# The distance table without its weight: each R tile multiplies for itself

## The chip, the cores and the metric

One core of a Trainium2 chip runs the whole program. The metric is the device time of one execution in microseconds (us); a profiled execution also gives the span from the first to the last instruction. TensorE (PE in the rows) does the matrix products and the transposes, VectorE is DVE, ScalarE is ACT, GpSimd is POOL, and SyncE (SP) issues nearly all transfers. PEld is TensorE's load of stationary operands.

## The reference, cut to what matters

Attention with a position bias that a small network computes, then two feed-forward blocks. Only the bias is touched here:

```python
rel = (pos[:, None] - pos[None, :]).astype(np.float32)
psi_rel = np.log1p(np.abs(rel))
psi_i = np.log1p(np.maximum(pos[:, None].astype(np.float32), 1.0))
x = (psi_rel / psi_i)[..., None]
h = np.maximum(x @ w1 + b1, 0.0)          # w1: 1 x 32, hidden units
bias = h @ w2                             # 32 x 8 heads
scores = scores + bias.transpose(2, 0, 1)[None, :, :, :]
```

There are 2 batches, 8 heads, 576 positions and head size 64. After the softmax and the product with v come two blocks on 1152 x 512 rows: 512 to 2048 to 512, and a gated one with 1536.

## The kernel before, in words

The hidden layer depends on the pair of positions only through the distance d, once it is multiplied by psi_i: max(w1·log1p(d) + psi_i·b1, 0). The table `T` (128 partitions x 576) holds log1p(d). Its partitions are 4 rows of positions x 32 hidden units. `w1c` is w1, one value per partition; a transpose on TensorE (`turned`) makes it, and four small products (`norms`) make psi_i·b1 for all 576 rows. `NB1` is minus that and `SC` is that.

The 576 rows are 36 groups of 16. A group n has four R tiles, each 128 x `reach(n)`, from 304 to 576 columns wide: VectorE makes 123 of the 144 tiles as max(T, NB1 column) and ScalarE makes 21 as Relu(T + SC column). GpSimd has a branch for it and gets none. `bias_mm` (B.n in the table of the order, tile `bps`) multiplies the four by w2, `bias_evac` divides by psi_i into `ev`, `bias_store` writes it to the DRAM tables `biasd`, and `bias_load` reads them back, skewed, as the `bias` tile of a unit of attention. The tables are used in the order c = 2, 1, 3, 4, 0, eight groups each (four for c = 4), so nothing of the first softmax starts until groups 16 to 23 are made, stored and loaded.

A unit u of attention is a pair of heads of a tile of 128 positions: scores (S.u, tile `s`), VectorE's sum with the bias and its minimum (line 472, tiles `e` and `m`), ScalarE's exponential (line 483), transposes (T.u, `tps`), copies (`et`) and the product with v (PV.u). A table, ORDER, fixes TensorE's order for all of this by hand, with "W" for matmuls of the identity that keep TensorE at work and have no use else. The order on VectorE, ScalarE and SP is left to a scheduler, whose estimate decides where it puts an instruction. `rawk`, `rawq` and `vs`/`v` are the loads of k, q and v, `kps`/`qps` the transposed k and q in PSUM, `kS` the copy of the former in SBUF.

In `tile_attention_ffn_kernel` the start reads:

```python
            nc.vector.tensor_copy(out=w1c, in_=turned[:, 0, :1])
            nc.vector.tensor_scalar_mul(T, T, w1c)
            nc.vector.tensor_scalar_mul(NB1, norms, -1.0)
            nc.scalar.copy(out=SC, in_=norms)
```

From about 130 us on the feed-forward blocks run; they have no part in the change.

Of the kernel before, what the change touches and what calls it, by code (L numbers as in the profile page):

```python
# [13 lines left out]
ACTF = mybir.ActivationFunctionType  # L14
ALU = mybir.AluOpType
# [53 lines left out]
def kernel(ctx, tc, q, k, v, w1, b1, w2, w_in, w_out, w_gate, w_val, w_out2, rms_g, dtab, ntab, itab, out):  # L69
    nc = tc.nc  # L70
# [21 lines left out]
    w1c = const.tile([128, 1], F32, name="w1c")  # L92
# [11 lines left out]
    def transpose(out, in_):  # L104
        n = in_.shape[0]
        nc.tensor.transpose(out, in_, ident[:n, :n])  # L106
# [143 lines left out]
    if True:  # L250
# [12 lines left out]
        T = smc.tile([128, S], F32, name="T")  # L263
        SC = smc.tile([128, 4 * NG], F32, name="SC")
        INV = smc.tile([128, NG], F32, name="INV")
        NB1 = smc.tile([128, 4 * NG], F32, name="NB1")
# [39 lines left out]
        def load_k(b, p, n):  # L306

            if b == 2:
                a = rawp.tile([128, H, D], F32, tag="rawl", name="rawl", bufs=1)
                for o in range(2):  # L310
                    nc.sync.dma_start(out=a[64 * o:64 * o + 64], in_=rows(k[o, :, 512:576, :]))
            else:
                a = rawp.tile([128, 4, 2, D], F32, tag="rawk", name="rawk", bufs=BUFS["rawk"])
                for h in range(2):
                    gate(a[:1, 0, h, :1], n)
                    nc.sync.dma_start(out=a[:, :, h], in_=k[b, 2 * p + h, :512, :].rearrange("(c s) d -> s c d", c=4))
                a = a.rearrange("p c h d -> p (c h) d")
            raw_t["k", b, p] = a
# [45 lines left out]
        def reach(n):  # L364

            return max(S - 16 * n, 16 * n + 16)

        def bias_R(n, x, engine):
            R = Rp.tile([128, S], F32, tag="R", name="R")
            R_t[n, x] = R  # L370
            R, src, col = R[:, :reach(n)], T[:, :reach(n)], slice(4 * n + x, 4 * n + x + 1)
            if engine == "A":
                nc.scalar.activation(out=R, in_=src, func=ACTF.Relu, scale=1.0, bias=SC[:, col])
            else:
                if engine == "P":
                    nc.gpsimd.tensor_scalar(out=R, in0=src, scalar1=3.4e38, scalar2=NB1[:, col], op0=ALU.min, op1=ALU.max)
                else:
                    nc.vector.tensor_scalar(out=R, in0=src, scalar1=NB1[:, col], scalar2=None, op0=ALU.max)  # L378

        def bias_mm(n):  # L380
            N = reach(n)
# [184 lines left out]
        def warm(n):  # L566

            if not pv_t:
                for z in range(n):
                    nc.tensor.matmul(warm_t[:, z % 4, :], lhsT=ident, rhs=ident, start=True, stop=True)  # L570

        with tc.manual_schedule():
            nc.sync.dma_start(out=T, in_=dtab.to_broadcast([128, S]))
            nc.scalar.dma_start(out=wr, in_=w1.rearrange("o (g k) -> o g k", g=1).to_broadcast([1, 4, 32]))
            nc.sync.dma_start(out=nr, in_=ntab.rearrange("(o g) t -> o g t", o=1))
            nc.scalar.dma_start(out=br, in_=b1.rearrange("(o k) -> o k", o=1))
            nc.sync.dma_start(out=w2s, in_=w2)
            nc.scalar.dma_start(out=INV, in_=itab.rearrange("g (o t) -> g o t", o=1).to_broadcast([16, 8, NG]))
            load_k(0, 0, None)
            load_k(2, 0, None)  # L580

            make_identity(nc, ident)
            nc.gpsimd.memset(W2b, 0.0)
            nc.vector.memset(nb1, 0.0)
            for b in range(B):
                for o in range(2):
                    (nc.gpsimd if b else nc.vector).memset(v4[b][64 * o:64 * o + 64, :, 1 - o, :], 0.0)
            nc.scalar.activation(out=nb1, in_=nb1, func=ACTF.Exp)
            warm(EARLY[0])
            turned = ps_t.tile([128, 4, 128], F32, tag="t", name="turned")  # L590
            transpose(turned[:, 0, :1], wr.rearrange("o g k -> o (g k)"))
            norms = ps_t.tile([128, 4 * NG], F32, tag="t", name="norms", padded_shape=[128, 512])
            for g in range(4):
                nc.tensor.matmul(norms[32 * g:32 * g + 32], lhsT=br, rhs=nr[:, g], start=True, stop=True)
            warm(EARLY[1])
            nc.vector.tensor_copy(out=w1c, in_=turned[:, 0, :1])
            nc.vector.tensor_scalar_mul(T, T, w1c)
            nc.vector.tensor_scalar_mul(NB1, norms, -1.0)
            nc.scalar.copy(out=SC, in_=norms)

# [22 lines left out]
        for i, n in enumerate(n for c in order for n in range(8 * c, min(8 * c + 8, NG))):  # L623
            g = group_key(i)
            z = "z" if i < 8 else ""
            R_eng[n] = "".join(sorted(START[i] if i < 8 else MID[i % len(MID)], key="PDA".index))
            for j, x in enumerate(sorted(range(4), key=lambda x: "PAD".index(R_eng[n][x]))):
                e = R_eng[n][x]
                at(g + (P[z + "rp"] if e == "P" else P[z + "ra"] if e == "A" else P[z + "rd"] * j), ("R", n, x), (), bias_R, n, x, e)
            at(g + P[z + "b"], ("B", n), [("R", n, x) for x in range(4)] + [("cc",)], bias_mm, n)  # L630
            o = 16 * n + 15
            for h, length in enumerate((o, S - o)):
                e = "D" if length <= P[z + "evd"] else "A"
                at(g + P[z + "ev"] + .001 * h, ("EV", n, h), [("B", n)], bias_evac, n, h, e)
            key = g + P[z + "ev"] + .001 + P[z + "st"]
            at(key, ("ST", n), [("EV", n, 0), ("EV", n, 1)], bias_store, n)
            c = n // 8
            stored_key[c] = max(stored_key.get(c, -99), key)
            nth[i] = n, key - 1e-5
# [352 lines left out]
```

## Time and profile before

| what | value |
|---|---|
| time, median of 3 runs | 632.74 us (631.61 to 634.47) |
| the profiled execution | 632.15 us |
| its span | 630.4 us |
| granted TensorE clock, mean | 0.998 |
| busy: PE, PEld | 620.1 us, 526.4 us |
| busy: DVE, ACT, POOL | 442.2 us, 352.3 us, 143.5 us |
| instructions | 11000 |

The span is 1.75 us shorter than the execution's time; what lies around it is the start and the end of the program. TensorE is counted busy nearly throughout, but a matmul that waits inside its pipeline is counted too, so a small wait shows in the starts of its neighbours rather than as idle time.

### The profile page before, as it was taken

To read this page: it belongs to the slowest core of one execution; us is meant where nothing else is said; L and a number is where in the kernel's file an instruction comes from. 1 tells how busy PE (TensorE), PEld (TensorE's weight loads), DVE (VectorE), ACT (ScalarE), POOL (GpSimd) and SP (SyncE) were. 2 spreads that over 40 slices of the span, in tenths; PEclk is the share of its full clock that TensorE was granted. 3 is DMA by queue.
4 is the path that set the end of the run, shared out by engine and by line. 5 is a ranking of instruction groups with operands and counts; after the bars stand their busy time and mean duration, and the time that the engine had idled before them with its cause. 6 is when DMAs were issued, how large, how long until landed. Compare 5 with 4: busy or idle time off the path is not lost.

```text
span 630.4 us, 11000 instructions
## 1 busy us (share of the span) xinstructions
PE 620.1 (98%) x4185; PEld 526.4 (84%) x4185; DVE 442.2 (70%) x820; ACT 352.3 (56%) x733; POOL 143.5 (23%) x114
## 2 busy tenths in 40 slices
PE   8999999999999999999999999999999999999996
PEld 4456766767779999999999898999999999999996
DVE  5967686547656998988826799878777652497712
ACT  6778877879775655555425555654444431254411
POOL 1000001101210433333300133423323330032500
PEclk9999999999999999999999999999999999999999
DMA  8999565378101433443300223534343430164201
GB/s 193 265 243 285 171 185 157 106 202 281 39 2 36 149 124 128 133 132 115 122 34 0 76 101 127 166 96 122 117 134 100 151 117 0 35 210 130 96 0 51
DMA packets 73569, 77.73 MB, mean 123 GB/s; under 512 B 31659, under 2 KB 58283, under 8 KB 73516
## 3 DMA queue, kind: packets, MB, share of 16 engines
q1 hardware_dynamic: 73362, 77.00, 40.8%
q8 instruction: 33, 0.54, 0.3%
q14 instruction: 20, 0.16, 0.1%
q10 hardware_dynamic: 154, 0.02, 0.0%
HBM read 63.76 MB, written 13.25 MB: 122 GB/s over the span
## 4 chain that ended last, share of the span: by engine, by line
PE 92%; DVE 3%; DMA 2%; ACT 1%; issue 1%; SPq 1%; DVEq 0%; ACTq 0%
PE h L777 40%; PE ya L822 18%; PE yb L822 9%; PE s L459 6%; PE pv L522 6%; PE tps L106 6%; PE bps L389 4%; DVE R L378 1%; DMA bias<-biasd 1%; PE rps L106 1%; PE qps L106 1%; PE xnT L106 1%; DMA T<-in_dtab_dram 1%; DMA rawq<-in_q_dram 1%; DVE wm L164 0%
## 5 line engine op out<-in xcount | busy, mean ns | idle before, releaser
L176 POOL TENSOR_TENSOR wl<-wm,wh 128x512 fp32r<-128x512 f32 x85 | 125.7, 1479 | 301.7 <-ACT wh L143 200.8
L168 DVE SCALAR_TENSOR_TENSOR wm<-raw,wm 128x512 int32<-128x512 int32 x85 | 121.5, 1430 | 0.9
L786 ACT CAST gh<-r 128x384 fp32r<-128x384 f32 x84 | 43.2, 514 | 112.4 <-DVE r L809 68.5
L777 PE MATMUL h<-nh,wh 128*128 128x384 f32 x288 | 97.3, 338 | 0.0
L777 PE MATMUL h<-nh,wl 128*128 128x384 f32 x288 | 96.7, 336 | 0.0
L777 PE MATMUL h<-nl,wh 128*128 128x384 f32 x288 | 96.4, 335 | 0.0
L472 DVE CUSTOM_DVE_ANT_0 e<-s,bias 128x576 f32<-128x576 f32 x72 | 51.9, 754 | 28.4 <-PE s L459 17.9
L483 ACT ACTIVATE e<-e,m 128x576 f32<-128x576 f32 x72 | 55.6, 775 | 17.9 <-DVE m L472 17.7
L777 PE MATMUL h<-xh,wh 128*128 128x384 f32 x192 | 65.4, 341 | 0.0
L777 PE MATMUL h<-xh,wl 128*128 128x384 f32 x192 | 64.7, 337 | 0.0
L777 PE MATMUL h<-xl,wh 128*128 128x384 f32 x192 | 64.4, 336 | 0.0
L809 DVE TENSOR_TENSOR r<-r,h 128x384 f32<-128x384 f32 x36 | 19.9, 553 | 63.3 <-PE h L777 63.3
L164 DVE SCALAR_TENSOR_TENSOR wm<-raw,wm 128x512 int32<-128x512 int32 x85 | 59.7, 704 | 2.8
L789 DVE TENSOR_TENSOR gl<-r,gh 128x384 fp32r<-128x384 f32 x84 | 46.6, 554 | 16.2 <-ACT gh L786 16.2
L154 ACT ACTIVATE wm<-raw 128x512 f32<-128x512 f32 x84 | 56.4, 673 | 0.8 <-DMA raw<-in_moe_w_val_dram 0.8
L777 PEld LDWEIGHTS h<-nh,wh 128*128 128x128 f32 x288 | 54.1, 188 | 2.3 <-DVE nl L886 0.9
L797 ACT ACTIVATE r<-h,half_c 128x384 f32<-128x384 f32 x48 | 27.8, 579 | 49.7 <-PE h L777 49.7
L777 PEld LDWEIGHTS h<-nl,wh 128*128 128x128 f32 x288 | 54.1, 188 | 1.4
L777 PEld LDWEIGHTS h<-nh,wl 128*128 128x128 f32 x288 | 54.0, 188 | 0.0
L805 ACT ACTIVATE r<-h 128x384 f32<-128x384 f32 x36 | 17.7, 493 | 64.9 <-PE h L777 64.9
L143 ACT CAST wh<-wm 128x512 fp32r<-128x512 f32 x85 | 52.3, 617 | 0.9 <-DVE wm L168 0.8
L378 DVE TENSOR_SCALAR R<-T,NB 128x336 f32<-128x336 f32 (+17 forms) x123 | 47.4, 448 | 4.6 <-PE bps L389 4.4
(109 smaller groups left out, 1103.5 us busy)
## 6 DMA issues: line engine op xcount, KB each, us to landing
raw<-in_moe_w_out_dram SPq DMA_DIRECT2D x33, 512.0 KB, 3.5
biasd<-ev SPq DMA_DIRECT2D x36, 295.5 KB, 3.8
raw<-in_moe_w_in_dram SPq DMA_DIRECT2D x18, 512.0 KB, 3.6
raw<-in_moe_w_gate_dram SPq DMA_DIRECT2D x18, 512.0 KB, 3.4
bias<-biasd SPq DMA_DIRECT2D x15, 576.0 KB, 4.7
raw<-in_moe_w_val_dram SPq DMA_DIRECT2D x16, 512.0 KB, 3.4
bias<-biasd SPq DMA_DIRECT2D x10, 288.0 KB, 4.1
rawk<-in_k_dram SPq DMA_DIRECT2D x16, 128.0 KB, 3.2
```

The lines of the kernel that those rows point to most:

```text
L106: nc.tensor.transpose(out, in_, ident[:n, :n])
L143: nc.scalar.copy(out=hi, in_=m)
L154: nc.scalar.activation(out=m, in_=raw[:, :, 1].bitcast(F32), func=ACTF.Abs, scale=held[0] if held else 2.0 ** -112)
L164: nc.vector.scalar_tensor_tensor(out=m, in0=raw[:, :, 0], scalar=29, in1=m, op0=ALU.logical_shift_right, op1=ALU.bitwise_or,)
L168: nc.vector.scalar_tensor_tensor(out=m, in0=raw[:, :, 1], scalar=-0x80000000, in1=m, op0=ALU.bitwise_and, op1=ALU.bitwise_or,)
L176: nc.gpsimd.tensor_tensor(out=lo, in0=m, in1=hi, op=ALU.subtract)
L378: nc.vector.tensor_scalar(out=R, in0=src, scalar1=NB1[:, col], scalar2=None, op0=ALU.max)
L472: nc.vector.tensor_tensor_reduce(out=e_t[u][:, a, :].rearrange("p (z j) -> p z j", z=2), in0=s[:, :, :SH], in1=bt[u][:, a, :].rearrange("p ...
L483: nc.scalar.activation(out=e_t[u][:, a, :], in_=e_t[u][:, a, :], func=ACTF.Exp, scale=-1.0, bias=m_t[t][:, h:h + 1], accum_out=sum_t[t][:, ...
L777: nc.tensor.matmul(ps, lhsT=w[wz][:, c * 128:(c + 1) * 128], rhs=x[xz][:, c, :], start=(i == 0), stop=(i == 11),)
L789: nc.vector.tensor_tensor(out=gl, in0=g, in1=gh, op=ALU.subtract)
L822: nc.tensor.matmul(y_t[ph, n, t], lhsT=g[gz][:, t * 128:(t + 1) * 128], rhs=w[wz], start=(f == 0 and i == 0), stop=(f == F - 1 and i == 2),)
```

## The change

The multiplication of the whole table by `w1c` at the start goes. Each R tile takes the product into its own instruction: on VectorE multiply by `w1c` and then the maximum with the NB1 column, both operands one value per partition; on ScalarE the scale of the activation is `w1c` instead of the constant 1. GpSimd's branch is written likewise, and is not used. Everything else is the same in the source.

```diff
             if engine == "A":
-                nc.scalar.activation(out=R, in_=src, func=ACTF.Relu, scale=1.0, bias=SC[:, col])
+                nc.scalar.activation(out=R, in_=src, func=ACTF.Relu, scale=w1c, bias=SC[:, col])
             else:
                 if engine == "P":
-                    nc.gpsimd.tensor_scalar(out=R, in0=src, scalar1=3.4e38, scalar2=NB1[:, col], op0=ALU.min, op1=ALU.max)
+                    nc.gpsimd.tensor_scalar(out=R, in0=src, scalar1=w1c, scalar2=NB1[:, col], op0=ALU.mult, op1=ALU.max)
                 else:
-                    nc.vector.tensor_scalar(out=R, in0=src, scalar1=NB1[:, col], scalar2=None, op0=ALU.max)
+                    nc.vector.tensor_scalar(out=R, in0=src, scalar1=w1c, scalar2=NB1[:, col], op0=ALU.mult, op1=ALU.max)
...
             nc.vector.tensor_copy(out=w1c, in_=turned[:, 0, :1])
-            nc.vector.tensor_scalar_mul(T, T, w1c)
             nc.vector.tensor_scalar_mul(NB1, norms, -1.0)
```

TensorE's order is the same to the row. VectorE, ScalarE and SP get another order in places. On VectorE, where the first softmax begins (line 472 is the sum with the bias, the row after it its minimum; NB_116 is `NB1`; kS_138 and kS_139 are batch 0 and 1), the program before has:

```order
22 L378 TENSOR_SCALAR R<-T,NB_116 128x352 x4
23 L378 TENSOR_SCALAR R<-T,NB_116 128x336 x3
24 L350 COPY kS_138<-kps 128x512
25 L378 TENSOR_SCALAR R<-T,NB_116 128x400 x2
26 L472 ISA e,m<-s,bias 128x576
27 L472 ISA m 128x1
28 L378 TENSOR_SCALAR R<-T,NB_116 128x400
29 L472 ISA e,m<-s,bias 128x576
```

and the changed program has, at the same place:

```order
21 L378 TENSOR_SCALAR R<-T,w1c,NB_116 128x352 x4
22 L378 TENSOR_SCALAR R<-T,w1c,NB_116 128x336 x3
23 L350 COPY kS_138<-kps 128x512
24 L472 ISA e,m<-s,bias 128x576
25 L472 ISA m 128x1
26 L378 TENSOR_SCALAR R<-T,w1c,NB_116 128x400
27 L472 ISA e,m<-s,bias 128x576
28 L472 ISA m 128x1
```

Two R tiles that stood ahead of the first sum with the bias now stand behind it.

On SP, around the last stores of the first bias table and its first loads (biasd_74 is the table c = 2, biasd_73 is c = 1; vs_140 and vs_141 are v of batch 0 and 1), the program before has:

```order
9 L330 DMA v_142<-in_v_dram 64x4x64
10 L316 DMA rawk<-in_k_dram 128x4x64 x2
11 L418 DMA biasd_74<-ev 16x8x591 x4
12 L316 DMA rawk<-in_k_dram 128x4x64 x2
13 L418 DMA biasd_74<-ev 16x8x591 x4
14 L330 DMA v_142<-in_v_dram 64x4x64
15 L316 DMA rawk<-in_k_dram 128x4x64 x4
16 L444 DMA bias<-biasd_74 128x576 x2
17 L444 DMA bias<-biasd_74 128x2x576 x2
```

and the changed program:

```order
9 L330 DMA v_142<-in_v_dram 64x4x64 x2
10 L316 DMA rawk<-in_k_dram 128x4x64 x2
11 L418 DMA biasd_74<-ev 16x8x591 x4
12 L316 DMA rawk<-in_k_dram 128x4x64 x2
13 L418 DMA biasd_74<-ev 16x8x591 x3
14 L330 DMA vs_141<-in_v_dram 128x4x64
15 L418 DMA biasd_74<-ev 16x8x591
16 L418 DMA biasd_73<-ev 16x8x591
17 L330 DMA vs_140<-in_v_dram 128x4x64
18 L316 DMA rawk<-in_k_dram 128x4x64 x4
19 L444 DMA bias<-biasd_74 128x576 x2
20 L444 DMA bias<-biasd_74 128x2x576 x2
```

One load of v moved far ahead, and two loads of v and the first store of the table c = 1 moved ahead of the k loads and of the first bias loads.

## Rows read from the trace of the kernel before

**Rows 1.** The page, busy time of each engine, share of the span, instructions.

```profile
PE 620.1 (98%) x4185; PEld 526.4 (84%) x4185; DVE 442.2 (70%) x820; ACT 352.3 (56%) x733; POOL 143.5 (23%) x114
```

**Rows 2.** The chain that ended last, 0 to 60 us: start, duration, what.

```profile
16.47 2.72 DVE R L378 x8
...
25.96 6.85 DMA bias<-biasd
...
32.94 0.76 DVE e L472
...
33.76 1.91 PE s L459 x8
```

**Rows 3.** Timeline of VectorE, 4 to 24 us: start, duration, instruction, idle before.

```profile
4.71 0.52 DVE L597 TENSOR_SCALAR T<-T,w1c 128x576 f32<-128x576 f32 x1 [0.45 <-DMA T<-in_dtab_dram]
5.15 0.30 DVE L598 TENSOR_SCALAR NB<-norms 128x144 f32<-128x144 f32 x1
...
7.68 1.94 DVE L378 TENSOR_SCALAR R<-T,NB 128x304 f32<-128x304 f32 x6 [0.66 <-PE bps L389]
11.40 0.69 DVE L350 COPY kS<-kps 128x512 f32<-128x512 f32 x1 [1.79 <-PE kps L106]
12.01 11.80 DVE L378 TENSOR_SCALAR R<-T,NB 128x336 f32<-128x336 f32 x35
```

**Rows 4.** Timeline of TensorE, 19 to 23 us.

```profile
19.32 1.45 PE L389 MATMUL bps<-R,W2b 128*32 128x400 f32 x8 [0.54 <-DVE R L378]
...
21.35 0.91 PE L389 MATMUL bps<-R,W2b 128*32 128x416 f32 x8
22.18 1.09 PE L106 MATMUL kps<-ident,rawk 128*128 128x128 f32 x8
```

**Rows 5.** VectorE by shape: count, busy, mean ns, idle before.

```profile
L378 DVE TENSOR_SCALAR R<-T,NB 128x576 f32<-128x576 f32 x7 | 3.3, 514 | 0.1
...
L378 DVE TENSOR_SCALAR R<-T,NB 128x304 f32<-128x304 f32 x6 | 1.9, 374 | 0.7 <-PE bps L389 0.7
```

**Rows 6.** VectorE line 163, a shift by an immediate: ns min/median/max.

```profile
L163 DVE TENSOR_SCALAR wm<-wm x85: 409/420/1105, 150.8 to 594.0; 128x512 int32<-128x512 int32 x85
```

**Rows 7.** ScalarE out of PSUM: scale by an immediate, by a column.

```profile
L359 ACT ACTIVATE q<-qps 128x512 f32<-128x512 f32 x7 | 4.2, 595 | 0.5 <-PE qps L106 0.5
...
L412 ACT ACTIVATE ev<-bps,INV 128x512 f32<-128x512 f32 x1 | 0.7, 665 | 0.0
```

**Rows 8.** Timeline of ScalarE, 5 to 12 us.

```profile
5.79 3.26 ACT L373 ACTIVATE R<-T,SC 128x320 f32<-128x320 f32 x7
...
10.97 0.60 ACT L359 ACTIVATE q<-qps 128x512 f32<-128x512 f32 x1 [0.17 <-PE qps L106]
```

**Rows 9.** Timeline of SP's queue, 20 to 25 us.

```profile
20.23 0.69 SPq L330 DMA_DIRECT2D v<-in_v_dram  x1
22.87 2.02 SPq L316 DMA_DIRECT2D rawk<-in_k_dram  x4
```

**Rows 10.** Windows before and after the end of the stores, us, busy of each engine, clock, DMA share, GB/s.

```profile
20.00:23.00 3.00, 3.00 (x26) 1.55 (x24) 3.00 (x9) 2.00 (x6) 0.00 (x0) 1.00 0.96 302
23.00:24.00 1.00, 0.92 (x11) 0.19 (x9) 1.00 (x4) 0.94 (x4) 0.00 (x0) 1.00 0.21 55
```

**Rows 11.** R tiles on VectorE by window: us, busy (count), clock, DMA share, GB/s.

```profile
60.00:70.00 10.00, 6.24 (x14) 1.00 1.02 321
...
80.00:90.00 10.00, 8.07 (x18) 1.00 0.66 190
```

**Rows 12.** Timelines behind these bursts: VectorE's sums, TensorE's next scores.

```profile
68.01 0.75 DVE L472 CUSTOM_DVE_ANT_0 e<-s,bias 128x576 f32<-128x576 f32 x1
...
69.68 1.24 PE L459 MATMUL s<-kS,q 64*128 64x288 f32 x8
...
90.13 0.75 DVE L472 CUSTOM_DVE_ANT_0 e<-s,bias 128x576 f32<-128x576 f32 x1
...
90.76 1.41 PE L459 MATMUL s<-kS,q 64*128 64x288 f32 x8
```

## The prediction

> **What bounds the kernel now.** I read the page first: TensorE is counted busy for 620.1 of 630.4 us [rows 1], so a change pays or costs only where it moves the instructions that TensorE waits for. The chain that ended last says where that is early on: up to 19 us it runs through R tiles on VectorE, then through TensorE and a load of the bias of 6.85 us, then VectorE's sum at 32.94, which lets TensorE's next scores start at 33.76 [rows 2]. The timeline of VectorE shows why. It waits 1.79 us for a transposed k, copies it at 11.40, and then makes 35 R tiles in 11.80 us without a gap [rows 3]. TensorE follows close behind: its products with 400 columns at 19.32 waited 0.54 us for an R tile, and those with 416 columns start at 21.35 [rows 4]. Those are tiles 22 to 24 and 25 to 28 of the 35 (before them stand 2 of 336 columns, 4 each of 352, 368 and 384, 3 of 368 and 4 of 384). From 33.76 on TensorE has nearly no idle time, and the R tiles left are made beside it.
>
> **The change part by part.** The first term is the multiplication that goes: one instruction of 0.52 us at 4.71. NB1 was made behind it from 5.15, so the R tiles can start at most 0.52 us earlier. This gives nothing. What it shortens ends in the idle 1.79 us ahead of the copy at 11.40 [rows 3], and that copy waits for k and not for the table. If that cover were gone, the gain would be at most these 0.52 us.
>
> The second term is the longer R tile on VectorE, 123 of them. No row has two column operands in one instruction, so I bound it. From 304 columns (374 ns) to 576 columns (514 ns) a tile grows by 140 ns over 272 columns, 0.515 ns per column [rows 5]. At 512 columns that line gives 481 ns with one column operand. Line 163, of the same 512 columns in SBUF, with an immediate instead, has a median of 420 ns [rows 6]. So a column operand costs about 61 ns. The lower bound for a second one is nothing, if both are fetched together; the upper one is 61 ns, plus half of the rate if the second operation halves it (the third rival). I take 60 ns: the nearest row prices an operand by itself, and nothing in the trace shows two fetched for the price of one. VectorE overlaps neighbours by the same 0.08 us whatever they are (the copy at 11.40 lasts 0.69 and the next tile starts 0.61 after it [rows 3]), so the 60 ns go into the distance from tile to tile in full.
>
> Where that lies: the six tiles from 7.68 take 0.36 us more, inside the 1.79 us of idle time. The copy at 11.40 stays where it is. Then tile 28 of the run that starts at 12.01 ends 28 x 0.060 = 1.7 us later, and with it the products with 416 columns [rows 3, 4]. What is late next: the transposes of k at 22.18 come behind them in TensorE's order, the four k loads at 22.87 wait for those to free their buffers, and the bias loads stand behind these on SP's queue [rows 4, 9]. So the load of 25.96, the sum of 32.94 and the scores of 33.76 [rows 2] all move by 1.7 us. Nothing absorbs it on the way, since this run of tiles is on the chain.
>
> The third term is later bursts, where TensorE has little idle time to give. Between 60 and 70 us there are 14 R tiles, 0.84 us more [rows 11]; the second sum behind them ends at 68.76 and TensorE's next scores start at 69.68 [rows 12], so 0.92 us of room covers that, barely. Between 80 and 90 us there are 18, 1.08 us more; the second sum behind them ends at 90.88, inside the group of scores that began at 90.76 and needs its buffer [rows 11, 12]. There is no room, so up to 1.1 us could come through. Other tiles and two waits of VectorE on TensorE stand in that burst, so I take 0.8, between 0 and 1.3 with the few tiles around 105 us.
>
> The fourth is ScalarE's 21 tiles. There a column operand for the scale shows as 665 against 595 ns, 70 ns [rows 7]. Seven of the tiles start at 5.79, so what follows comes 0.5 us later at most; ScalarE waits 0.17 us ahead of the copy of q at 10.97 [rows 8], and the rest delays only work that stands ahead of VectorE's later run. The other 14 are spread over 100 us. I take nothing, and 0.5 as the upper end.
>
> The fifth is the order. On SP, two loads of v (128 x 256 x 4 bytes, 0.13 MB each) and one store of bias (16 x 8 x 591 x 4 bytes, 0.30 MB) now stand ahead of the k loads and so of the first bias loads, 0.56 MB in all. SP sits idle from 20.92 to 22.87 [rows 9], which covers their issue. The transfers themselves find the engines at 0.21 in the microsecond after 23 us, and at 302 GB/s before it [rows 10]: 0.79 x 302 GB/s takes 0.24 MB, and the other 0.32 MB take 1.1 us. With the k loads 1.7 us later by the second term that is covered. If the second term is nothing, it is not. On VectorE two R tiles stand behind the first sum now instead of ahead of it. That sum waits for the bias load, so this at most hides their own time. I take nothing for both. No wait is new: `w1c` is written before NB1 is, and every R tile waited for NB1 already.
>
> The sum against the profiled execution's own time, 632.15: 632.15 - 0 + 1.7 + 0.8 + 0 + 0 = 634.65, say 634.7 us. That execution lies 0.6 us under the median of the runs shown, 632.74; I leave the forecast at 634.7, 0.3% over the median.
>
> **The rivals.** First, the second operand is free on VectorE. For it: two operands of one instruction may be fetched side by side, and the trace says nothing against it. Then only the fifth term is left, 0 to 1.1 us, and the time is 632.2 to 633.3, the same as before.
>
> Second, the late tiles cost more than I count. In the bursts of rows 11 VectorE's sums, ScalarE's exponentials and TensorE's scores wait for each other in a ring, and a delay in it can come back once per unit instead of once per burst. If both bursts pass on their 0.84 and 1.08 us and the ring doubles what comes through, that is 3.8 us beside the 1.7, near 637.5. Against it speaks the room of 0.92 us at 68.76 [rows 12].
>
> Third, the tile with two operations falls to half its rate. This ends on the other side, slower than a measurement's noise. By the row of 0.515 ns per column it would add as much again: with 378 columns in the mean of the first 28 tiles, 0.195 us each on top of 0.060, so 7.1 us at 33.76 instead of 1.7, and in the bursts 14 x 0.33 - 0.92 = 3.7 and 18 x 0.35 = 6.3 us. That is 639 with nothing of the bursts and 649 with all; about 644. It decides from 0.05 us per tile on top of the operand, since 28 of those make 1.4 us more at the first softmax and 634.7 passes 635.9. The rows have only one operation at this rate, so they can't exclude it.
>
> [...] No run here shows a wide tile with two operations.
>
> Fourth, faster by more than the noise. The sum ahead of two R tiles and the earlier store of the table c = 1 would have to clear more than 3.2 of the 10.3 us in which TensorE is idle in the whole span [rows 1]. The order on TensorE is fixed and the bias load is behind the k loads in both programs, so I see no place for it.
>
> **How the numbers follow.** The forecast 0.55, the free operand 0.24, the later waits 0.11, the halved rate 0.07, faster 0.03. A measurement here can tell about 0.5%, 3.2 us, from no change: 629.6 to 635.9. The range starts at 631.7, under the free operand by half a microsecond for the spread of the runs, and ends at 638.5, which takes in the upper ends of the third and fourth terms (634.7 + 0.5 + 0.5) and the second rival. It leaves out the halved rate, the faster case and the edges of the others, about 2 in 10. Of the forecast a fifth lies over 635.9 (0.11), with most of the second rival (0.09) and all of the third (0.07): slower 0.27. Faster 0.03, the same 0.70.
>
> **What would show it.** R tiles on VectorE of 434 ns at 304 columns and 574 ns at 576 columns, with the same slope, and the run behind the copy at 11.40 growing from 11.80 to about 13.9 us, show the second term. The products with 416 columns should start near 23.0, the k loads near 24.5, the bias load land near 34.5, and the scores of 33.76 come near 35.4. Behind that, the distance from these scores to the first matmul of the feed-forward block should grow by less than 1.3 us. Tiles as long as before show the first rival; then the load of the bias tells whether the moved transfers cost anything. A steeper slope than 0.515 ns per column shows the third. The prediction is wrong if TensorE's waits grow at a place that holds no R tile, for then it is the order on SP or ScalarE that decides and not the tile.

## The result, and the profile after

The changed kernel takes 636.8 us in the median of four runs (636.26 to 637.55), against 632.62 us for the kernel before beside it: a ratio of 1.0067, with a 95% interval of 1.0047 to 1.0087. It is 4.2 us slower. The profiled execution took 636.82 us with a span of 635.0 us, 4.6 us more than the span of before.

The page, busy time of each engine:

```profile
PE 619.8 (98%) x4185; PEld 526.6 (83%) x4185; DVE 449.3 (71%) x819; ACT 353.8 (56%) x733; POOL 143.3 (23%) x114
```

TensorE is as busy as before [rows 1], so all of the loss is new idle time on it. VectorE works 7.1 us more. By shape (count, busy us, mean ns, idle before):

```profile
L378 DVE TENSOR_SCALAR R<-T,w1c,NB 128x576 f32<-128x576 f32 x7 | 3.9, 608 | 0.0
...
L378 DVE TENSOR_SCALAR R<-T,w1c,NB 128x304 f32<-128x304 f32 x6 | 2.3, 434 | 0.6 <-PE bps L389 0.6
```

A tile of 304 columns takes 434 instead of 374 ns [rows 5]. The mean of the seven of 576 columns is raised by one long tile; those of 560 columns, with a mean of 565 ns (506 before), are 59 ns longer. Over all widths the means differ by 57 to 62 ns at 14 of 18; the other four, between 52 and 94, hold single long tiles. The slope over the columns is unchanged (0.512 ns per column from 304 to 560 columns, 0.516 before), so this is a price per instruction. Timeline of VectorE (start, duration, what, idle before):

```profile
4.80 0.31 DVE L597 TENSOR_SCALAR NB<-norms 128x144 f32<-128x144 f32 x1 [0.55 <-PE norms L594]
...
11.74 0.69 DVE L350 COPY kS<-kps 128x512 f32<-128x512 f32 x1 [1.97 <-PE kps L106]
12.35 13.85 DVE L378 TENSOR_SCALAR R<-T,w1c,NB 128x336 f32<-128x336 f32 x35
...
65.67 3.58 DVE L378 TENSOR_SCALAR R<-T,w1c,NB 128x512 f32<-128x512 f32 x7
69.17 0.30 DVE L410 TENSOR_SCALAR ev<-bps,INV 128x95 f32<-128x95 f32 x1
```

The 35 tiles take 13.85 instead of 11.80 us [rows 3], 59 ns more each. The wait ahead of the copy is still there, longer by 0.18 us. Timeline of TensorE:

```profile
23.14 1.07 PE L389 MATMUL bps<-R,W2b 128*32 128x416 f32 x8
24.14 1.09 PE L106 MATMUL kps<-ident,rawk 128*128 128x128 f32 x8
...
30.21 0.63 PE L106 MATMUL kps<-ident,rawk 128*128 128x128 f32 x4 [0.59 <-DMA rawk<-in_k_dram]
...
32.73 0.75 PE L459 MATMUL s<-kS,q 64*128 64x288 f32 x2 [0.56 <-DVE m L472]
33.80 1.23 PE L459 MATMUL s<-kS,q 64*128 64x288 f32 x6 [0.33 <-DVE m L472]
...
36.16 1.77 PE L459 MATMUL s<-kS,q 64*128 64x288 f32 x8
...
69.62 0.63 PE L106 MATMUL rps<-ident,rb 128*128 128x128 f32 x4 [0.49 <-DVE ev L410]
...
72.55 0.66 PE L106 MATMUL tps<-ident,e 128*128 128x128 f32 x4 [0.36 <-ACT et L504]
...
89.91 1.18 PE L389 MATMUL bps<-R,W2b 128*32 128x288 f32 x16 [0.68 <-DVE ev L410]
...
112.24 1.15 PE L389 MATMUL bps<-R,W2b 128*32 128x280 f32 x16 [0.94 <-ACT ev L412]
```

The products with 416 columns start 1.8 us later than in [rows 4], and the scores of 33.76 [rows 2] are now those of 36.16, 2.4 us later. Behind them the slip grows at four waits of TensorE: at 69.62, 89.91 and 112.24 for an evacuation `ev` of the bias products, and at 72.55 for ScalarE's copy `et`. The three of `ev` in the trace of before:

```profile
66.74 0.63 PE L106 MATMUL rps<-ident,rb 128*128 128x128 f32 x4
...
85.80 1.18 PE L389 MATMUL bps<-R,W2b 128*32 128x288 f32 x16
...
107.57 3.73 PE L389 MATMUL bps<-R,W2b 128*32 128x280 f32 x48 [0.44 <-ACT ev L412]
```

So the slip grows from 2.4 us to 2.9 at the first, about 3.4 behind the wait for `et` (the scores of 69.68 [rows 12] come at 73.13), 4.1 and 4.7 us, and stays there. SyncE's queue before, the same queue after, VectorE's first sum with the bias before, and pieces of the chain that ended last after:

```profile
25.00 2.03 SPq L444 DMA_DIRECT2D bias<-biasd  x4
```

```profile
23.63 0.37 SPq L330 DMA_DIRECT2D vs<-in_v_dram  x1
24.83 2.89 SPq L316 DMA_DIRECT2D rawk<-in_k_dram  x4
27.81 1.99 SPq L444 DMA_DIRECT2D bias<-biasd  x4
```

```profile
28.48 0.75 DVE L472 CUSTOM_DVE_ANT_0 e<-s,bias 128x576 f32<-128x576 f32 x1
```

```profile
27.81 4.07 DMA bias<-biasd
31.91 0.76 DVE e L472
```

The k loads are issued 2.0 us later than in [rows 9], and the four bias loads behind them 2.8 us later. The chain runs through a bias load as before, but not through the same one of the four. In [rows 2] it is the third, issued at 25.96, for which VectorE's third sum waits until 32.94. Here it is the first, issued at 27.81: the first sum, which ran at 28.48 before, waits for it until 31.91. TensorE's scores at 32.73 and 33.80 wait for the minima `m` of the first two sums, and those of 36.16 follow without another wait. TensorE's transposes of k wait for their load too, until 30.21, but the scores behind them then wait 0.56 us more for `m`.

About 0.3 us of these differences need not be an effect of the change. TensorE's transposes of q wait for a load, and start at 10.30 in the profiled execution of before, at 10.64 in this one, and between 10.46 and 10.95 in every experiment, with the old tiles and order too.

### The profile page after: what moved, and what is told of

It reads as the page before. It is cut to its first block, busy times and chain, and to the rows that moved or that the text cites. A ratio compares the mean times of both kernels' runs of the same rounds, so it can differ in the third digit from the quotient of the medians.

```text
span 635.0 us, 11006 instructions
## 1 busy us (share of the span) xinstructions
PE 619.8 (98%) x4185; PEld 526.6 (83%) x4185; DVE 449.3 (71%) x819; ACT 353.8 (56%) x733; POOL 143.3 (23%) x114
## 4 chain that ended last, share of the span: by engine, by line
PE 90%; DVE 3%; ACT 3%; DMA 2%; issue 1%; SPq 1%; DVEq 0%; ACTq 0%
PE h L776 40%; PE ya L821 18%; PE yb L821 9%; PE s L459 6%; PE pv L522 6%; PE tps L106 5%; PE bps L389 3%; ACT ev L412 1%; ACT e L483 1%; DVE e L472 1%; PE qps L106 1%; DMA rawq<-in_q_dram 1%; DMA bias<-biasd 1%; PE xnT L106 1%; PE rps L106 1%
## 5 line engine op out<-in xcount | busy, mean ns | idle before, releaser
L472 DVE CUSTOM_DVE_ANT_0 e<-s,bias 128x576 f32<-128x576 f32 x72 | 51.9, 754 | 26.6 <-PE s L459 17.5
L378 DVE TENSOR_SCALAR R<-T,w1c,NB 128x336 f32<-128x336 f32 (+17 forms) x123 | 55.1, 512 | 3.7 <-PE bps L389 3.6
```

What stands on the lines that cost most here:

```text
L378: nc.vector.tensor_scalar(out=R, in0=src, scalar1=w1c, scalar2=NB1[:, col], op0=ALU.mult, op1=ALU.max)
L472: nc.vector.tensor_tensor_reduce(out=e_t[u][:, a, :].rearrange("p (z j) -> p z j", z=2), in0=s[:, :, :SH], in1=bt[u][:, a, :].rearrange("p ...
```

## The experiments

Four theories. **Operand:** the second column operand costs 60 ns on each of VectorE's tiles, and that is the loss. **Operation:** the second operation costs it. **Order:** the rows that the scheduler moved cost it. **ScalarE:** its scale column costs it. All kernels were timed in five rounds. Differences are given by the ratio to the kernel before, times 632.6 us. This ratio is not the quotient of the two medians and can differ from it by some 0.1%.

To part price from order, I wrote the steps of the attention stage into a table in the order in which the engines ran them (a gated load and `x_ri` are cut into their single instructions). With the table of one kernel and the tile code of the other, every engine runs the rows of one in the order of the other.

```diff
-        with tc.manual_schedule(engines={mybir.EngineType.PE}):
-            emit(P["man"], 100)
+        with tc.manual_schedule():
+            for z in STEPS:
...
+                fn(*args)
+                done.add(name)
```

**The control**, the old tiles in the old order. 

> The kernel before, with the steps of its attention stage written out in the order in which its engines ran them, so that no scheduler chooses: every engine has the same rows as before. A control for the next two. Both theories: the time of the kernel before, 632.6 us, within 0.3%. If it is further off, writing the order out costs something of its own (extra waits), and the next two are read against this kernel alone.

Measured: 632.61 us, ratio 1.0000 (0.9984 to 1.0015). Writing the order out costs nothing that shows.

**The new tiles in the old order.**

```diff
-                nc.scalar.activation(out=R, in_=src, func=ACTF.Relu, scale=1.0, bias=SC[:, col])
+                nc.scalar.activation(out=R, in_=src, func=ACTF.Relu, scale=w1c, bias=SC[:, col])
...
-                    nc.vector.tensor_scalar(out=R, in0=src, scalar1=NB1[:, col], scalar2=None, op0=ALU.max)
+                    nc.vector.tensor_scalar(out=R, in0=src, scalar1=w1c, scalar2=NB1[:, col], op0=ALU.mult, op1=ALU.max)
...
-            nc.vector.tensor_scalar_mul(T, T, w1c)
```

> The changed kernel's instructions (distance table not multiplied, each R tile with the weight's column), in the kernel before's order on VectorE, ScalarE, SyncE and TensorE. Theory, that the second column operand's 60 ns on each VectorE tile is the whole loss: 636 to 637.5 us, all of the +4.2. Rival, that the scheduler's new order (bias loads later on SyncE, two ScalarE copies behind the exponentials) makes the later half: 634.5 to 635.2, only the +2.4 of the first 34 us.

Measured: 636.01 us, ratio 1.0057 (1.0040 to 1.0073), 3.6 us (2.5 to 4.6). The tiles alone make nearly the whole loss. TensorE's timeline at the scores of 33.76 and the products of 107.57:

```profile
36.33 1.24 PE L467 MATMUL s<-kS,q 64*128 64x288 f32 x8
...
111.80 3.73 PE L397 MATMUL bps<-R,W2b 128*32 128x280 f32 x48 [0.63 <-ACT ev L420]
```

**The old tiles in the new order**: the control with the other table. 

> The other way round: the kernel before's instructions (table multiplied once, one column operand) in the changed kernel's order. Theory (the operand is the loss): 632.2 to 633.4 us, no difference from before. Rival (the order makes the later half): 634.5 to 635.5. If order and operand each cost only together, both of these kernels come out near 633 and neither theory holds.

Measured: 636.28 us, ratio 1.0057 (1.0039 to 1.0076), 3.6 us (2.5 to 4.8). So the order alone makes nearly the whole loss as well, though part of it goes with TensorE's clock: in four of its six executions the mean granted clock is 0.993 to 0.996, and they took 636.05 to 638.26 us; the two at 1.00 took 634.75 and 635.31. My theory and its rival both missed this: each was to get its part, and each gets nearly all of it. SyncE's queue and TensorE's timeline in this kernel:

```profile
23.50 0.93 SPq L322 DMA_DIRECT2D rawk<-in_k_dram  x2
24.52 0.53 SPq L426 DMA_DIRECT2D biasd<-ev  x1
25.14 0.54 SPq L338 DMA_DIRECT2D vs<-in_v_dram  x1
25.78 1.47 SPq L322 DMA_DIRECT2D rawk<-in_k_dram  x2
```

```profile
30.94 0.63 PE L106 MATMUL kps<-ident,rawk 128*128 128x128 f32 x4 [2.53 <-DMA rawk<-in_k_dram]
...
35.99 1.51 PE L467 MATMUL s<-kS,q 64*128 64x288 f32 x8
```

No tile is longer here, and still the transposes of k wait 2.53 us for a load, because the last k load is issued at 26.6 instead of 24.4 us; the bias loads stand behind it in the queue. The scores of 33.76 come at 35.99.

**Two operations with one column operand**, in the old order.

```diff
-                    nc.vector.tensor_scalar(out=R, in0=src, scalar1=NB1[:, col], scalar2=None, op0=ALU.max)
+                    nc.vector.tensor_scalar(out=R, in0=src, scalar1=1.0, scalar2=NB1[:, col], op0=ALU.mult, op1=ALU.max)
```

> The kernel before with each VectorE R tile as two operations, a product with the constant 1.0 and then the maximum with the column; the table is still multiplied once. One column operand as before, same order on every engine. Theory (the column operand costs 60 ns, the operation nothing): 632.3 to 633.0 us, and tiles of 374 ns at 304 columns. Rival, that the second operation is what costs 60 ns: 636 to 637 us, and tiles of 434 ns.

Measured: 632.55 us, ratio 1.0000 (0.9986 to 1.0015). By shape:

```profile
L378 DVE TENSOR_SCALAR R<-T,NB 128x576 f32<-128x576 f32 x7 | 3.3, 513 | 0.1
...
L378 DVE TENSOR_SCALAR R<-T,NB 128x304 f32<-128x304 f32 x6 | 1.9, 372 | 0.8 <-PE bps L389 0.8
...
L373 ACT ACTIVATE R<-T,SC 128x512 f32<-128x512 f32 x1 | 0.7, 718 | 0.0
```

513 and 372 ns are the old times [rows 5]. The second operation adds nothing to them, so the 57 to 62 ns come with the column operand. The slope is the old one too: 0.518 ns per column with two operations, 0.515 with one [rows 5].

Where do operand and order cost? The next four cut both at the scores of 33.76.

**The operand on VectorE's first 55 tiles alone, and on its last 68 alone** (U is the scaled table, T the unscaled one; for the second, `> 55`).

```diff
-            nc.vector.tensor_scalar_mul(T, T, w1c)
+            nc.vector.tensor_scalar_mul(U, T, w1c)
...
+                    if len(vec) <= 55:
+                        nc.vector.tensor_scalar(out=R, in0=raw, scalar1=w1c, scalar2=NB1[:, col], op0=ALU.mult, op1=ALU.max)
+                    else:
+                        nc.vector.tensor_scalar(out=R, in0=src, scalar1=NB1[:, col], scalar2=None, op0=ALU.max)
```

> The old order on every engine; the first 55 R tiles of VectorE (those made before its first sum) take the unscaled table and the weight's column, the other 68 and ScalarE's 21 the scaled table as before. Theory, that the operand's loss has two places, about 2.2 us up to the scores of 33.76 and about 1.9 us in the bursts behind 60 us: 634.5 to 635.3 us, scores of 33.76 2 us later and no further slip behind. Rival, that the later slip only follows from the early one: 636 us, as with all tiles.

> The same with the other 68 VectorE tiles instead (those made after the first sum). Theory of two places: 634.0 to 634.8 us, scores of 33.76 unmoved, the products of 66.74, 85.80 and 107.57 later by 0.6 to 1.9 us. Rival (the later slip only follows from the early one): 632.3 to 633 us. My forecast's third term would say 633.3.

Measured, the first 55: 634.20 us against 632.83, ratio 1.0010 (0.9997 to 1.0023), 0.6 us (-0.2 to 1.5). TensorE's timeline:

```profile
23.16 1.07 PE L403 MATMUL bps<-R,W2b 128*32 128x416 f32 x8
...
36.08 1.91 PE L473 MATMUL s<-kS,q 64*128 64x288 f32 x8 [1.02 <-DVE m L486]
```

In the profiled execution the scores come 2.3 us later, up to 0.4 of it by the load of q, and nothing is added behind them. The chain that ended last runs as in [rows 2], with the same bias load issued 2.0 us later:

```profile
27.95 7.18 DMA bias<-biasd
35.26 0.76 DVE e L486
```

By the ratio the early part is smaller than that, and not safely told from nothing. The granted clock accounts for much of this. Of the 35 executions of before timed beside this kernel, 23 have a mean granted clock of 0.998 or more and took 631.49 to 633.30 us; the other 12 took 633.45 to 635.44. Of this kernel's 12 only one is below 0.998, and the other eleven took 633.15 to 635.16. Among those at 0.998 or more, the medians differ by 1.7 us.

Measured, the last 68: 634.72 us, ratio 1.0026 (1.0011 to 1.0041), 1.6 us (0.7 to 2.6); 2.0 us among the executions at 0.998 or more. VectorE's and TensorE's timelines:

```profile
62.75 4.03 DVE L390 TENSOR_SCALAR R<-T,w1c,NB 128x512 f32<-128x512 f32 x8
66.70 0.30 DVE L424 TENSOR_SCALAR ev<-bps,INV 128x95 f32<-128x95 f32 x1
```

```profile
67.15 0.63 PE L106 MATMUL rps<-ident,rb 128*128 128x128 f32 x4 [0.62 <-DVE ev L424]
...
86.58 1.18 PE L403 MATMUL bps<-R,W2b 128*32 128x288 f32 x16 [0.29 <-DVE ev L424]
...
109.06 3.73 PE L403 MATMUL bps<-R,W2b 128*32 128x280 f32 x48 [0.63 <-ACT ev L426]
```

Here the scores of 33.76 stand at 33.38, 0.4 us early. Then `rps` starts 0.4 us late, the products of 85.80 come 0.8 and those of 107.57 come 1.5 us late: 0.8 + 0.4 + 0.7, 1.9 us in all. The later slip needs no early one. The rival, that the late slip follows from the early one, falls.

**The new order up to the scores of 33.76 alone, and behind them alone** (old tiles; the table is put together from the two). 

> The kernel before's instructions; the changed kernel's order up to the scores of 33.76, the old one behind: only SyncE's queue and the tiny copies that gate two loads differ (two loads of v stand ahead of two k loads and two bias stores). Theory, that these loads delay the k loads behind them: 634.5 to 635.2 us, k loads landing 2 to 3 us later. Rival, that SyncE's order costs nothing, and the loss is ScalarE's and VectorE's order later: 632.3 to 633 us.

> The kernel before's instructions; the old order up to the scores of 33.76, the changed kernel's behind. Theory (SyncE's order early 2.2 us, the rest 1 us): 633.2 to 634.0 us. Rival (the loss is ScalarE's and VectorE's order behind 34 us): 635 to 636.3 us.

Measured, up to 34 us: 634.91 us, ratio 1.0022 (1.0008 to 1.0037), 1.4 us (0.5 to 2.3). Only SyncE's queue and two gating copies differ there, so the moved transfers do cost: 1.3 us between the five executions at 0.998 or more and those of before. In the other seven the clock is lower (0.993 to 0.997). Measured, from 34 us on: 634.38 us, ratio 1.0020 (1.0007 to 1.0033), 1.3 us (0.4 to 2.1). ScalarE's and TensorE's timelines in the second kernel:

```profile
70.42 0.24 ACT L512 COPY et<-tps 128x128 f32<-128x128 f32 x1
70.56 0.58 ACT L555 COPY rt<-rps 128x512 f32<-128x512 f32 x1
71.04 1.07 ACT L512 COPY et<-tps 128x512 f32<-128x512 f32 x2
```

```profile
70.71 0.66 PE L106 MATMUL tps<-ident,e 128*128 128x128 f32 x4 [0.19 <-ACT et L512]
...
87.78 1.18 PE L397 MATMUL bps<-R,W2b 128*32 128x288 f32 x16 [0.38 <-DVE ev L418]
```

ScalarE's copy `rt` now stands behind two exponentials and a copy `et`, and TensorE's transposes wait for `et`. The products of 85.80 wait for VectorE's `ev`, the place at which they also wait for the longer tiles.

By their ratios the halves add up to 2.2 us for the tiles and 2.7 for the order, where the whole is 3.6 each time. By the executions at 0.998 or more it is 1.7 and 2.0, 3.7 us, for the tiles, where the whole is 3.5 (five executions), and 1.3 and 1.9, 3.2 us, for the order, where the whole is 2.5 (two executions). So nothing shows that the halves feed each other.

**ScalarE's 21 tiles alone** (edit as above, on ScalarE's line). 

> The old order; only ScalarE's 21 R tiles take the unscaled table with the weight's column as their scale, VectorE's 123 the scaled table. Forecast's fourth term: nothing, at most 0.5 us, so 632.3 to 633.3 us; the tiles longer by 70 to 100 ns. Rival, that ScalarE's tiles are part of the loss: 634 us or more.

Measured: 632.46 us against 632.26, ratio 0.9997 (0.9986 to 1.0009). By shape:

```profile
L382 ACT ACTIVATE R<-T,SC,w1c 128x512 f32<-128x512 f32 x1 | 0.8, 807 | 0.0
```

807 against 718 ns in the kernel with two operations; 89 to 98 ns over the shapes, 92 in the mean, and no time lost.

**The multiplication taken out alone.**

```diff
-            nc.vector.tensor_scalar_mul(T, T, w1c)
```

> The old order and the old tiles without the multiplication of the table, so that the output leaves out the weight. Forecast's first term: it ends in idle time, 632.3 to 633.0 us, and VectorE's wait ahead of its copy at 11.40 longer by what was saved. Rival, that the 0.5 us come through: 632.0 us or less in the median, which five rounds may just tell.

Measured: 632.89 us, ratio 1.0005 (0.9992 to 1.0018). VectorE's timeline:

```profile
12.35 0.69 DVE L358 COPY kS<-kps 128x512 f32<-128x512 f32 x1 [2.97 <-PE kps L106]
```

VectorE is through with the tiles ahead of this copy at 9.38 instead of 9.61, and what is saved ends in the wait for k. (Most of the wait's 1.2 us over [rows 3] is not that: 0.5 come from the load of q and some from TensorE's transposes at half speed, which the last section shows.)

**Four buffers for k**, with the old tiles and with the new ones, both in the old order but for two k loads that stand one bias store earlier on SyncE.

```diff
-BUFS = dict(rawk=3, rawq=2,
+BUFS = dict(rawk=4, rawq=2,
```

> The kernel before with four buffers instead of three for the loads of k (the steps in the old order; on SyncE two k loads then stand one bias store earlier). Theory, that the loads at 22.87 wait for transposes that wait for VectorE's tiles, and that the scores of 33.76 hang on that: 631 to 632 us. Rival, that the bias loads behind them need the last bias store at 24.5 anyway and the queues are full there: 632.3 to 633 us, or slower where the earlier k loads delay the bias stores.

> The changed kernel's instructions in the old order with four k buffers, so that the four k loads no longer wait for transposes behind VectorE's R tiles. If the early loss goes through those k loads, as my second term had it, it shrinks: 634.2 to 635.2 us, the later 1.9 us being what stays. If it goes through the products and the bias stores alone: 635.6 to 636.5 us, as with three buffers.

Measured: 632.59 us with the old tiles, ratio 1.0001 (0.9989 to 1.0012), no faster version. With the new tiles 635.62 us, ratio 1.0048 (1.0031 to 1.0064), 3.0 us (2.0 to 4.0) against 3.6 with three buffers. The intervals overlap, so whether the early loss goes through the wait for a k buffer stays open. TensorE's timeline with four buffers and the new tiles has the scores of 33.76 at 34.99:

```profile
34.99 1.24 PE L467 MATMUL s<-kS,q 64*128 64x288 f32 x8
```

The 36.33 with three buffers belongs to an execution with slow transposes (last section) and is no fair mark. The early tiles alone are one: their products with 416 columns start at 23.16, those with four buffers at 23.18, and their scores come at 36.08. That speaks for it by 1.1 us, in one execution of each. The times do not: among the executions at 0.998 or more the loss is 3.4 us with four buffers and 3.5 with three.

## Why the prediction was right, and where it was mis-sized

The forecast, 634.7 us in 631.7 to 638.5, holds the measured 636.8 us, and the likeliest case was the right one: the operand costs 60 ns and passes through where TensorE waits for VectorE. The size was too small, a loss of 2.5 us forecast and 4.2 measured. By the prediction's own line of 635.9 us the result is slower, which had 0.27, and not the same, which had 0.70. That the range holds it is in part luck: its upper end was drawn for the second rival, whose ring is not what happens, and without that rival the upper ends of the terms give 635.7.

**First term, the multiplication: nothing.** Shown within the noise, by the kernel without it (0.9992 to 1.0018).

**Second term, 60 ns per VectorE tile, 1.7 us at the scores of 33.76.** The price is right: 57 to 62 ns at nearly every width, the same slope, and the run of 35 tiles at 13.85 us where 13.9 was forecast. The products with 416 columns were to start near 23.0 and did at 23.14; the k loads near 24.5, and they did at 24.83. The way behind them was the forecast one, through a bias load and a sum to the scores. With the early tiles in the old order it is even the same load: it lands at 35.13 for the forecast 34.5, and the scores come at 36.08 for 35.4. In the changed kernel the first bias load takes its place, and the scores come at 36.16. Up to 0.4 of these gaps is the load of q. At an undisturbed clock the early tiles cost 1.7 us, as forecast; by the ratio over all executions it is 0.6 (-0.2 to 1.5).

**Third term, later bursts, 0.8 us, "between 0 and 1.3": the step that failed by its size.** The last 68 tiles alone cost 1.6 us (0.7 to 2.6), and their trace shows 1.9. I had read the room at the second sum, 0.92 us at 68.76 [rows 12], and let it cover the burst at 60 to 70 us. But another wait ends first: VectorE's small evacuation `ev`, queued behind 12 of the tiles, ended at 66.59 in the trace of before and TensorE's `rps` started at 66.74:

```profile
66.29 0.30 DVE L410 TENSOR_SCALAR ev<-bps,INV 128x95 f32<-128x95 f32 x1
```

The same 0.15 us lies between the two where TensorE waits for it, with the late tiles longer (67.00 and 67.15) and in the changed kernel (69.47 and 69.62), so there was no room. The first burst gave 0.8 us for the nothing that I had put there. The second gave 0.4 at `ev` and 0.7 more until 107.57, 1.1 for 0.8.

**Fourth term, ScalarE: nothing.** Shown. The price was 92 ns and not 70, which is hidden all the same.

**Fifth term, the order: nothing.** Up to the scores it held, and by the reason given: with the longer tiles they come at 36.16 in the new order and at 36.08 in the old one (the early tiles alone), so the moved loads are covered. Behind them it did not hold. From the scores to the products of 107.57 the slip grows by 2.3 us in the changed kernel and by 1.7 with the same tiles in the old order, and the wait of 72.55 for ScalarE's `et` stands at a place that holds no R tile, which is the prediction's own sign that the order decides there. Tiles and order each cost 0.57% alone and 0.67% (0.47 to 0.87) together, not 1.14%. But the price without that cover was wrong. I gave 0 to 1.1 us for SyncE's queue and nothing for the rest; measured were 1.4 us (0.5 to 2.3) up to 34 us, and 1.3 us (0.4 to 2.1) from ScalarE's and VectorE's order behind, which I had not priced. With a free operand, the first rival, the new order would have made 636.3 us and not 632.2 to 633.3.

The second rival, later waits that cost more than counted, named the right place for what was missing, but its ring that doubles each delay is not what the traces show: each slip happens once and stays. The half rate and the faster case are refuted by the tile times and by the ratio. The 0.07 for the half rate was my estimate: no run ahead of the result had an R tile with two operations. With two operations the tiles then took 0.518 ns per column, where half the rate would have been 1.03 (twice 0.515 [rows 5]).

## What to carry to other kernels

Give a per-partition column that takes the place of an immediate its own price in each instruction, here 60 ns on VectorE and 92 ns on ScalarE; a second operation in the same instruction cost nothing here (372 ns for 374 at 304 columns). Where a queue gets longer, look for room at every instruction queued behind it that another engine waits for, and above all at the small ones, not only at the large one that ends the burst. Where an automatic scheduler sits between the edit and the engines, freeze the old order and try price and order apart: here each made nearly the whole loss, and they did not add. And look at the granted clock of every execution before a small difference is called nothing: the early tiles' 0.6 us by the ratio were 1.7 us where the clock stayed up.

## What the runs showed of the hardware

A second column operand on a VectorE tile costs as much again as the first by the nearest rows: at 512 columns 420 ns with an immediate (another operation, [rows 6]), 481 by the line of one column [rows 5], 541 by the same line with two. Measured on the tiles, the second column operand costs 57 to 62 ns on VectorE, and on ScalarE a column in place of the constant scale costs 92 ns in the mean.

In four of the profiled executions TensorE's transposes stand 0.21 instead of 0.11 us apart between about 10.5 and 13.5 us, behind its wait for q; in two of the four the granted clock shows it (0.50 from 12.0 to 13.5 us), and for the other two the trace has no clock that early. A second such stretch, between 30 and 40 us, stands in two of the four, the control and the kernel with the new order up to 34 us. Windows of the latter (busy us of TensorE, its weight loads, VectorE, ScalarE and GpSimd, then the granted clock):

```profile
12.00:13.50 1.50, 1.50 (x10) 0.44 (x10) 1.30 (x4) 0.02 (x1) 0.00 (x0) 0.50 1.30 214
...
30.00:35.00 5.00, 3.22 (x15) 3.25 (x16) 1.78 (x5) 2.25 (x6) 0.00 (x0) 0.67 0.96 337
```

The granted clock was 0.50 after an idle time of 1.97 us for q; the changed kernel waited 1.70 us at the same place and kept 1.00. The two without a clock there waited 1.15 and 1.21, so the length of this wait alone does not decide. The work behind it was 1.3 us late at 15.4 us, 0.4 of it by the load of q. The clock fell again, to 0.67 in the mean from 30 to 35 us, after 2.68 us of waiting for k, at a place where the kernel with the whole new order waited 2.53 us and kept 1.00. A lower mean clock comes in some executions of most kernels but not equally often: it is below 0.998 in 22 of 87 executions of before, in 11 of 18 of the two kernels that move the early loads, and in 1 of 12 with the early tiles. So I used the traces for where a wait is. What it costs I took from the rounds, with the clock of each execution beside them.
